# A spectral filter gated with a token MLP: reordered stages, smaller transforms, a hardware GELU

## The chip, the cores and the metric

The kernel runs on one core of a Trainium2 chip. TensorE (PE in the profile) multiplies matrices into PSUM, VectorE (DVE), ScalarE (ACT) and GpSimd (POOL) work on elements, and SyncE (SP) only issues transfers between HBM and SBUF. Each engine takes its own queue in order. The metric is the device time of one execution in microseconds: 221.72 us is the median of 4 runs of the kernel before (220.94 to 899.45).

## The reference

The input x has 2048 tokens of 512 channels. Two branches are mixed by a gate:

```
g = sigmoid(sum(x * gate_w, channels))
a = irfft2(rfft2(x) * (w_r + i w_i))                        # 2048 x 512
h = layernorm(x, channels)
b = (gelu(h^T w1 + b1) w2 + b2)^T                           # 2048 -> 1792 -> 2048, along the tokens
out = g * a + (1 - g) * b
```

`gelu` is the tanh approximation. All inputs and the output are bf16.

## The kernel before

P = 128 partitions; the tokens make NB = 16 blocks of 128, F = 1792 makes NFT = 14 column tiles.

**Branch b (dense).** Layer norm on DVE: `bn_stats` and `bn_aggr` for each block (L296, L297), one square root on ACT for all blocks (L299), a reciprocal, and a scaling for each block in place (L302). The first product (L344) makes 14 tiles `u`, each of 16 matmuls of 128 x 512 in a PSUM bank of a ring of two. GELU is done by hand: ACT adds the bias (L347), DVE forms u(u^2 + c) in two operations (L349, L350), ACT takes a sigmoid (L352), DVE multiplies (L353). The second product (L459) makes 16 tiles `yb` of 14 matmuls each, and ACT scales and biases them by 1 - g into `tbv` (L461).

**Branch a (spectral).** The two-dimensional transform is cut into stages:
- f1 (L313, L315): the real transform over the 512 channels as a product with a table `tf1`, real and imaginary part in two banks, 4 matmuls each per block. A column 256 of the table carries `gate_w`, so the gate's sums come out of the same matmuls (L319).
- a DFT of 16 over the token blocks on DVE (`fft16`): two rounds of radix-4 butterflies of one group at a time (L67 to L84), with twiddles between them (L91 to L99).
- f3 (L377 to L380): a DFT of 128 within the blocks, 4 matmuls of 256 columns for each of the 16 e, with `tce`.
- the filter (L392 to L395), four DVE operations for each e, and a small correction for the packed column (channel frequency 0 and 256 share one), which needs a permutation on TensorE (L418, L420).
- i1 (L437 to L440): the inverse DFT of 128, 8 matmuls of 128 columns for each e, with `tice`; then the inverse `fft16`; then ya (L489): the inverse over the channels, 4 matmuls of 512 columns for each block; DVE mixes it with `tbv` (L495) and the block is stored (L497).

**Tables.** `tf1`, `tce`, `tice` and `tg` are made on the chip: POOL writes index ramps, DVE multiplies them and masks the product to the period (L222), ACT takes the sine (L43).

**Order.** All transfers are issued on one SyncE queue. A planner that runs when the kernel is built orders each engine's instructions, the first in the program having priority, with later work filling gaps that it expects; on the chip the orders are fixed. A tile asks a pool for a buffer: seven "planes" of 16 KB per partition hold the large tensors in turn, PSUM has rings of two banks called pA, pB and acc. A tile that takes a buffer over waits until the last reader of the tile before it is done.

Of the kernel before, what the change touches and what calls it, by code (L numbers as in the profile page):

```python
# [9 lines left out]
Alu = mybir.AluOpType  # L10
BF16 = mybir.dt.bfloat16
F32 = mybir.dt.float32

P = 128
# [5 lines left out]
NDT = 4  # L20
F = 1792
NFT = 14
PI_BIAS = -3.1415925

GELU_C3 = 2.0 * np.sqrt(2.0 / np.pi) * 0.044715
GELU_C22 = 1.0 / 0.044715


class KernelBuilder:
    def __init__(self, ctx, tc, dbg=None):  # L30
        self.ctx = ctx
        self.tc = tc
        self.nc = tc.nc
        self.dbg = dbg or {}
        self.c_pibias = None

    def dbg_out(self, key, src_ap):
        if key in self.dbg:
            self.nc.sync.dma_start(out=self.dbg[key], in_=src_ap)

    def sin_table(self, out_ap, arg_ap, n_period):
        np_ = arg_ap.shape[0]
        self.nc.scalar.activation(  # L43
            out_ap, arg_ap, ActF.Sin, bias=self.c_pibias[0:np_], scale=2.0 * np.pi / n_period
        )


def fft16(nc, pool, in_acc, a_acc, t_acc, out_acc, inverse, tmp_shape_full, tmp_shape_half,
          eng_add=None, eng_mul=None):
    add_eng = eng_add or (lambda i: nc.vector)  # L50
    mul_eng = eng_mul or (lambda i: nc.vector)
    cnt = [0]

    def nxt():
        cnt[0] += 1
        return cnt[0]

    def bfly(us, ys):
        p = pool.tile(tmp_shape_full, BF16, tag="ffp", name="fft_p")
        q = pool.tile(tmp_shape_full, BF16, tag="ffq", name="fft_q")  # L60
        r = pool.tile(tmp_shape_full, BF16, tag="ffr", name="fft_r")
        s = pool.tile(tmp_shape_full, BF16, tag="ffs", name="fft_s")

        def half(t, comp):
            return t[:, comp] if len(tmp_shape_full) == 3 else t[:, :, comp]

        add_eng(nxt()).tensor_add(p[:], us[0][0], us[2][0])  # L67
        add_eng(nxt()).tensor_add(q[:], us[1][0], us[3][0])
        add_eng(nxt()).tensor_sub(r[:], us[0][0], us[2][0])
        add_eng(nxt()).tensor_sub(s[:], us[1][0], us[3][0])  # L70
        add_eng(nxt()).tensor_add(ys[0][0], p[:], q[:])
        add_eng(nxt()).tensor_sub(ys[2][0], p[:], q[:])
        r_re, r_im = half(r, 0), half(r, 1)
        s_re, s_im = half(s, 0), half(s, 1)
        if not inverse:
            add_eng(nxt()).tensor_add(ys[1][1], r_re, s_im)
            add_eng(nxt()).tensor_sub(ys[1][2], r_im, s_re)
            add_eng(nxt()).tensor_sub(ys[3][1], r_re, s_im)
            add_eng(nxt()).tensor_add(ys[3][2], r_im, s_re)
        else:  # L80
            add_eng(nxt()).tensor_sub(ys[1][1], r_re, s_im)
            add_eng(nxt()).tensor_add(ys[1][2], r_im, s_re)
            add_eng(nxt()).tensor_add(ys[3][1], r_re, s_im)
            add_eng(nxt()).tensor_sub(ys[3][2], r_im, s_re)  # L84

    def twiddle(src, dst, m):
        theta = 2.0 * np.pi * m / 16.0
        c = float(np.cos(theta))
        s = float(-np.sin(theta)) if not inverse else float(np.sin(theta))
        if m % 16 == 4:  # L90
            mul_eng(nxt()).tensor_scalar_mul(dst[1], src[2], -s)  # L91
            mul_eng(nxt()).tensor_scalar_mul(dst[2], src[1], s)
            return
        t1 = pool.tile(tmp_shape_half, BF16, tag="tw1", name="tw_t1")
        t2 = pool.tile(tmp_shape_half, BF16, tag="tw2", name="tw_t2")
        mul_eng(nxt()).tensor_scalar_mul(t1[:], src[2], s)
        add_eng(nxt()).scalar_tensor_tensor(dst[1], src[1], c, t1[:], op0=Alu.mult, op1=Alu.subtract)
        mul_eng(nxt()).tensor_scalar_mul(t2[:], src[2], c)
        add_eng(nxt()).scalar_tensor_tensor(dst[2], src[1], s, t2[:], op0=Alu.mult, op1=Alu.add)  # L99

    for r in range(4):
        us = [in_acc(4 * m + r) for m in range(4)]
        ys = [a_acc(4 * r + k1) for k1 in range(4)]
        bfly(us, ys)
    for r in range(1, 4):
        for k1 in range(1, 4):
            twiddle(a_acc(4 * r + k1), t_acc(3 * (r - 1) + (k1 - 1)), r * k1)
    for k1 in range(4):
        us = []
        for r in range(4):  # L110
            if r == 0 or k1 == 0:
                us.append(a_acc(4 * r + k1))
            else:
                us.append(t_acc(3 * (r - 1) + (k1 - 1)))
        ys = [out_acc(k1 + 4 * k2) for k2 in range(4)]
        bfly(us, ys)
# [3 lines left out]
def kernel(  # L120
# [12 lines left out]
    dbg=None,  # L133
    stop_after=None,
):
    kb = KernelBuilder(ctx, tc, dbg)
# [4 lines left out]
    planes = ctx.enter_context(tc.tile_pool(name="planes", bufs=7))  # L141
    tbl = ctx.enter_context(tc.tile_pool(name="tbl", bufs=1))
    small = ctx.enter_context(tc.tile_pool(name="small", bufs=1))
    psum = ctx.enter_context(tc.tile_pool(name="psum", bufs=2, space=bass.MemoryType.PSUM))

    def plane_tile(shape, name):
        return planes.tile(shape, BF16, tag="plane", name=name)

    consts = small.tile([P, 8], F32, name="consts")
    nc.vector.memset(consts[:, 0:1], PI_BIAS)  # L150
    nc.vector.memset(consts[:, 1:2], 1e-5)
    kb.c_pibias = consts[:, 0:1]
    c_eps = consts[:, 1:2]

    xn = plane_tile([P, NB, D], "xn")
    nc.sync.dma_start(out=xn[:], in_=x2.rearrange("(b a) d -> a b d", a=P))
    xt = plane_tile([P, NDT, S], "xt")
    xr = x2.rearrange("s (dt p) -> s dt p", p=P)
    for dt in range(NDT):
        nc.sync.dma_start(out=xt[:, dt], in_=xr[:, dt], transpose=True)  # L160
    wrp = planes.tile([P, NE, 258], BF16, tag="plane", name="wrp")
    wip = planes.tile([P, NE, 258], BF16, tag="plane", name="wip")
    nc.sync.dma_start(out=wrp[:, :, 0:257], in_=A_w_r.rearrange("(c e) l -> c e l", e=NE))
    nc.sync.dma_start(out=wip[:, :, 0:257], in_=A_w_i.rearrange("(c e) l -> c e l", e=NE))
    b1b = small.tile([P, NFT], BF16, name="b1b")
    nc.sync.dma_start(out=b1b[:], in_=B_b1.rearrange("(ft f) -> f ft", f=P))
    b1f = small.tile([P, NFT], F32, name="b1f")
    nc.vector.tensor_copy(b1f[:], b1b[:])
    b2b = small.tile([P, NB], BF16, name="b2b")
    nc.sync.dma_start(out=b2b[:], in_=B_b2.rearrange("(b a) -> a b", a=P))  # L170
    b2f = small.tile([P, NB], F32, name="b2f")
    nc.vector.tensor_copy(b2f[:], b2b[:])

    tf1 = tbl.tile([P, NDT, 2, 257], BF16, name="tf1")
    tce = tbl.tile([P, 3, NE, P], BF16, name="tce")
    tice = tbl.tile([P, 3, NE, P], BF16, name="tice")
    tg = tbl.tile([P, 2, 2, D], BF16, name="tg")
    pmA = tbl.tile([P, P], F32, name="pmA")
    pmB = tbl.tile([P, P], F32, name="pmB")
    nc.vector.memset(tf1[:, :, 1, 256], 0.0)  # L180
    nc.sync.dma_start(out=tf1[:, :, 0, 256], in_=gate_w.rearrange("(dt p) -> p dt", p=P))
    with tc.tile_pool(name="tgen", bufs=1) as tgp:
        I32 = mybir.dt.int32
        lam_row = tgp.tile([P, L], F32, name="lam_row")
        nc.gpsimd.iota(lam_row[:], pattern=[[1, L]], base=0, channel_multiplier=0,
                       allow_small_or_imprecise_dtypes=True)
        a_row = tgp.tile([P, P], F32, name="a_row")
        nc.gpsimd.iota(a_row[:], pattern=[[1, P]], base=0, channel_multiplier=0,
                       allow_small_or_imprecise_dtypes=True)
        d_row = tgp.tile([P, D], F32, name="d_row")  # L190
        nc.gpsimd.iota(d_row[:], pattern=[[1, D]], base=0, channel_multiplier=0,
                       allow_small_or_imprecise_dtypes=True)
        d_col4 = tgp.tile([P, NDT], F32, name="d_col4")
        nc.gpsimd.iota(d_col4[:], pattern=[[P, NDT]], base=0, channel_multiplier=1,
                       allow_small_or_imprecise_dtypes=True)
        lam_col2 = tgp.tile([P, 2], F32, name="lam_col2")
        nc.gpsimd.iota(lam_col2[:], pattern=[[P, 2]], base=0, channel_multiplier=1,
                       allow_small_or_imprecise_dtypes=True)
        ce16 = tgp.tile([P, NE], F32, name="ce16")
        nc.gpsimd.iota(ce16[:], pattern=[[1, NE]], base=0, channel_multiplier=16,  # L200
                       allow_small_or_imprecise_dtypes=True)
        pcol = tgp.tile([P, 1], F32, name="pcol")
        nc.gpsimd.iota(pcol[:], pattern=[[0, 1]], base=0, channel_multiplier=1,
# [17 lines left out]
        def and_sin(dst_bf16, arg_i32, n_period):  # L221
            nc.vector.tensor_single_scalar(arg_i32, arg_i32, n_period - 1, op=Alu.bitwise_and)  # L222
            kb.sin_table(dst_bf16, arg_i32, n_period)
# [306 lines left out]
```

## Time and profile before

The profiled execution took 899.45 us, the other three 220.94 to 222.04. Both a matmul's length and TensorE's share are those of the 899.45 us execution.

| | value |
|---|---|
| time, median of 4 | 221.72 us |
| span of the profiled execution | 897.4 us |
| TensorE busy, matmuls | 837.6 us, 826 recorded |
| DVE busy, instructions | 161.1 us, 515 |
| ACT busy, instructions | 78.3 us, 124 |
| moved by DMA | 23.23 MB |
| first steady matmuls | 56 us after the start |

A group line reads: line, engine, operation, output<-input, shape, count, then busy time and mean ns of one, then the idle time of the engine just before and what ended it. A timeline line has start, length, engine, line, operation, and what it waited for in brackets. Busy lengths of neighbours on DVE overlap a little, so the cost of one in a dense stretch is the distance of two starts.

### The profile page before, as it was taken

What the parts mean: (1) busy time and instruction counts of PE and PEld (TensorE: products, weight loads), DVE (VectorE), ACT (ScalarE), POOL (GpSimd) and SP (SyncE); (2) the same over time, 40 slices, a digit from 0 to 9 for tenths busy, and PEclk for the clock granted to TensorE, in tenths of its full rate; (3) what the DMA queues carried; (4) which work ended last, traced back from release to release, by engine and by line L of the source; (5) the groups of instructions that cost most, each with busy time, mean ns of one, the idle gap of its engine ahead of it and who ended that gap; (6) DMA issues with size and microseconds to landing.
All of it is one profiled execution on the core that took longest, in us unless ns stands there. A gap on an engine that the chain in (4) does not pass through costs nothing.

```text
span 897.4 us, 2500 instructions
## 1 busy us (share of the span) xinstructions
PE 837.6 (93%) x826; PEld 268.1 (30%) x840; DVE 161.1 (18%) x515; ACT 78.3 (9%) x124; POOL 3.8 (0%) x13
## 2 busy tenths in 40 slices
PE   0289999999999999999999999999999999999998
PEld 0044442222222222222443556522222222222221
DVE  7641111111111111110332000570000000001111
ACT  1330010000000000000111112100000000000000
POOL 1000000000000000000000000000000000000000
DMA  9630000101010101000000100011010110000000
GB/s 230 134 93 0 1 0 0 47 0 47 0 47 0 47 0 47 0 1 0 0 0 0 42 0 0 1 41 34 7 41 0 41 42 0 0 0 18 23 29 23
DMA packets 50139, 23.23 MB, mean 26 GB/s; under 512 B 13264, under 2 KB 50128, under 8 KB 50128
## 3 DMA queue, kind: packets, MB, share of 16 engines
q1 hardware_dynamic: 50128, 23.09, 10.1%
q8 instruction: 6, 0.10, 0.0%
q14 instruction: 5, 0.04, 0.0%
HBM read 18.89 MB, written 2.10 MB: 23 GB/s over the span
## 4 chain that ended last, share of the span: by engine, by line
PE 93%; SPq 3%; DVE 1%; issue 1%; ACT 1%; DMA 0%; DVEq 0%
PE u L344 32%; PE yb L459 32%; PE ya L489 9%; PE f1im L315 5%; PE f1re L313 4%; SPq L160 2%; PE i1bank L437 1%; PE i1bank L438 1%; PE f3bank L377 1%; PE i1bank L440 1%; PE f3bank L380 1%; PE f3bank L379 1%; PE i1bank L439 1%; PE f3bank L378 1%; DMA tf<-in_gate_w_dram 0%
## 5 line engine op out<-in xcount | busy, mean ns | idle before, releaser
L459 PE MATMUL yb<-glv,w2t 128*128 128x512 bf16 x216 | 294.1, 1705 | 4.7 <-issue 4.7
L344 PE MATMUL u<-xn,w1t 128*128 128x512 bf16 x219 | 291.8, 1707 | 4.7 <-issue 4.7
L344 PEld LDWEIGHTS <-w1t 128*128 128x128 bf16 x224 | 72.6, 324 | 221.6 <-issue 221.6
L459 PEld LDWEIGHTS <-w2t 128*128 128x128 bf16 x224 | 73.0, 326 | 198.6 <-issue 198.1
L313 PE MATMUL f1re<-tf,xt 128*128 128x257 bf16 x64 | 60.9, 1037 | 42.5 <-DMA tf<-in_gate_w_dram 31.0
L489 PE MATMUL ya<-tg,zt 128*128 128x512 bf16 x63 | 84.1, 1707 | 0.9 <-issue 0.9
L495 DVE SCALAR_TENSOR_TENSOR ot<-ya,g,tbv 128x512 bf16<-128x512 f32 x16 | 12.0, 751 | 282.1 <-PE ya L489 282.1
L315 PE MATMUL f1im<-tf,xt 128*128 128x256 bf16 x64 | 61.3, 1041 | 0.0
L349 DVE TENSOR_TENSOR p<-ubt 128x512 bf16<-128x512 bf16 x14 | 6.0, 426 | 246.5 <-ACT ubt L347 246.5
L489 PEld LDWEIGHTS <-zt 128*128 128x128 bf16 x64 | 20.5, 320 | 64.0 <-issue 64.0
L313 PEld LDWEIGHTS <-xt 128*128 128x128 bf16 x64 | 19.5, 307 | 64.0 <-DMA tf<-in_gate_w_dram 31.0
L347 ACT ACTIVATE ubt<-u,b1f 128x512 bf16<-128x512 f32 x14 | 9.6, 688 | 258.0 <-PE u L344 258.0
L461 ACT ACTIVATE tbv<-yb,ombb,omg 128x512 bf16<-128x512 f32 x16 | 12.4, 778 | 221.4 <-PE yb L459 221.4
L315 PEld LDWEIGHTS <-xt 128*128 128x128 bf16 x64 | 20.3, 318 | 22.1 <-issue 21.6
L437 PE MATMUL i1bank<-tice,y 128*128 128x128 bf16 x32 | 22.2, 694 | 2.3 <-ACT vp L442 1.9
L440 PE MATMUL i1bank<-tice,y 128*128 128x128 bf16 x32 | 23.0, 720 | 0.0
L439 PE MATMUL i1bank<-tice,y 128*128 128x128 bf16 x32 | 22.9, 714 | 0.0
L438 PE MATMUL i1bank<-tice,y 128*128 128x128 bf16 x32 | 22.7, 709 | 0.0
L442 ACT ACTIVATE vp<-i1bank,wlam 128x256 bf16<-128x256 f32 x32 | 13.4, 471 | 80.5 <-PE i1bank L440 80.5
L318 DVE CAST xdt<-f1im 128x256 bf16<-128x256 f32 x16 | 6.8, 424 | 62.4 <-PE f1im L315 62.4
L377 PE MATMUL f3bank<-fu,tce 128*128 128x256 bf16 x16 | 16.8, 1047 | 0.9 <-ACT xs L381 0.9
L378 PE MATMUL f3bank<-fu,tce 128*128 128x256 bf16 x16 | 16.8, 1047 | 0.0
(170 smaller groups left out, 324.2 us busy)
## 6 DMA issues: line engine op xcount, KB each, us to landing
w2t<-in_B_w_dram SPq DMA_DIRECT2D x8, 896.0 KB, 5.2
w1t<-in_B_w_dram SPq DMA_DIRECT2D x7, 1024.0 KB, 6.0
xn<-in_A_x_dram SPq DMA_DIRECT2D x1, 2048.0 KB, 8.4
out_dram<-ot SPq DMA_DIRECT2D x16, 128.0 KB, 1.7
wrp<-in_A_w_r_dram SPq DMA_DIRECT2D x1, 1028.0 KB, 6.7
wip<-in_A_w_i_dram SPq DMA_DIRECT2D x1, 1028.0 KB, 9.9
xt<-in_A_x_dram SPq DMA_TRANSPOSE x4, 6.0
b1b<-in_B_b_dram SPq DMA_DIRECT2D x1, 3.5 KB, 9.3
```

The costliest lines, as they stand in the source:

```text
L160: nc.sync.dma_start(out=xt[:, dt], in_=xr[:, dt], transpose=True)
L313: nc.tensor.matmul(pre[:, 0:257], lhsT=lhsT, rhs=tf1[:, dt, 0, :], start=(dt == 0), stop=(dt == NDT - 1))
L315: nc.tensor.matmul(pim[:, 0:L], lhsT=lhsT, rhs=tf1[:, dt, 1, 0:L], start=(dt == 0), stop=(dt == NDT - 1))
L344: nc.tensor.matmul(u[:], lhsT=w1t[:, b, q * P:(q + 1) * P], rhs=xn[:, b, :], start=(b == 0), stop=(b == NB - 1))
L377: nc.tensor.matmul(bank[:, 0:L], lhsT=tce[:, 0, e, :], rhs=ure, start=True, stop=False)
L378: nc.tensor.matmul(bank[:, 0:L], lhsT=tce[:, 1, e, :], rhs=uim, start=False, stop=True)
L437: nc.tensor.matmul(bank[:, c0:c0 + P], lhsT=blk_re, rhs=tice[:, 0, e, :], start=True, stop=False)
L438: nc.tensor.matmul(bank[:, c0:c0 + P], lhsT=blk_im, rhs=tice[:, 2, e, :], start=False, stop=True)
L439: nc.tensor.matmul(bank[:, c0 + P:c0 + 2 * P], lhsT=blk_re, rhs=tice[:, 1, e, :], start=True, stop=False)
L440: nc.tensor.matmul(bank[:, c0 + P:c0 + 2 * P], lhsT=blk_im, rhs=tice[:, 0, e, :], start=False, stop=True)
L459: nc.tensor.matmul(yb[:], lhsT=w2t[:, ft, q2 * P:(q2 + 1) * P], rhs=glv[:, ft, :], start=(ft == 0), stop=(ft == NFT - 1))
L489: nc.tensor.matmul(ya[:], lhsT=zt[:, lt, b, comp, :], rhs=tg[:, lt, comp, :], start=(i == 0), stop=(i == 3))
```

## The change

The kernel is rewritten along the same stages; the purpose is less work on TensorE and DVE, and an earlier start. What it does:

- **Head.** x is loaded in four pieces, and the first six column tiles of w1 right after the first piece. Layer norm goes block by block, with a square root for each block, and the six tiles accumulate in six banks at once, block by block as they are normed. The transposed x for f1 comes after these loads.
- **f1** uses the symmetry of the transform: sums and differences of the two channel halves (`xf`) give even and odd frequencies, so that a block needs 4 matmuls of 256 columns. Evictions alternate between ACT and DVE. ya uses the same symmetry: even and odd parts in the two halves of a bank, ACT scales them by the gate, DVE adds and subtracts.
- **The gate** has its own sums: DVE multiplies x with a broadcast `gate_w`, ACT adds up along the channels; the sigmoid is taken as a tanh.
- **GELU** is one ACT activation per tile.
- **fft16** works on four groups at a time, with whole-tile operations of 2048 elements, and folds some twiddles into the butterflies. The filter works on four e at a time.
- **f3** and **i1** use wider matmuls: one of 512 and two of 256 columns for an e, and 4 of 256 for an e in i1.
- **Tables**: the products of ramps for `tce` and `tice` are made on POOL in quarters. The masks stay on DVE, the sines on ACT.
- **Buffers**: each large tensor has a fixed plane; `vp` takes the plane of `hn`, `wri` that of the table ramp `rec`. The dense product has six banks, everything else shares two. Weights of both products share four buffers.

The core of the diff:

```diff
-    psum = ctx.enter_context(tc.tile_pool(name="psum", bufs=2, space=bass.MemoryType.PSUM))
+    psum = ctx.enter_context(tc.tile_pool(name="psum", bufs=6, space=bass.MemoryType.PSUM))
+    home = {"x": 0, "fa": 0, "xs": 0, "ia": 0, "hn": 1, "vp": 1, "zt": 1, "xt": 2, "xdt": 2, "fu": 2, "ap": 2,
+            "marg": 3, "xf": 3, "y": 3, "rec": 4, "wri": 4, "marg3": 5, "gl": 5, "prod": 6, "tbv": 6}
...
+    for b0, b1 in ((0, 2), (2, 6), (6, 11), (11, 16)):
+        nc.sync.dma_start(out=x[:, b0:b1], in_=xv[:, b0:b1])
+        if b0 == 0:
+            load_w1a(0)
+    for g in range(1, 4):
+        load_w1a(g)
...
+    u1 = [mm_bank(f"u1_{ft}") for ft in range(FT1)]
+    for b in range(NB):
+        nc.vector.bn_stats(out=stats[:, b, :], in_=x[:, b, :])
+        nc.vector.bn_aggr(out=mv[:, b, :], in_=stats[:, b, :])
+        sq = nc.scalar.activation(rstd[:, b:b + 1], mv[:, b, 1:2], ActF.Sqrt, bias=consts[:, 1:2], scale=1.0)
+        nc.vector.reciprocal(rstd[:, b:b + 1], rstd[:, b:b + 1])
+        nc.vector.tensor_scalar(hn[:, b, :], x[:, b, :], mv[:, b, 0:1], rstd[:, b:b + 1],
+                                op0=Alu.subtract, op1=Alu.mult)
+        for ft in range(FT1):
+            nc.tensor.matmul(u1[ft][:], lhsT=w1a[b // 4][:, b % 4, ft * P:(ft + 1) * P], rhs=hn[:, b, :],
+                             start=(b == 0), stop=(b == NB - 1))
+    with tc.issue_after(sq.ins):
+        nsin(tf[:, :, :, 0, :], m1c.rearrange("p k (t i) -> p k t i", t=2), 512)
...
+        nc.gpsimd.tensor_scalar(m2[:, es], rec[:, es], dcol[:, 0:1], 0.0, op0=Alu.mult, op1=Alu.add)
+        nc.gpsimd.tensor_scalar(m2c[:, es], rec[:, es], dcol[:, 0:1], 1536.0, op0=Alu.mult, op1=Alu.add)
...
+        nc.vector.tensor_add(xf[:, 0, :, hs], xt[:, 0:2, hs], xt[:, 2:4, hs])
+        nc.vector.tensor_sub(xf[:, 1, :, hs], xt[:, 0:2, hs], xt[:, 2:4, hs])
...
-            ubt = gwork.tile([P, D], BF16, tag="ub", name="ubt")
-            nc.scalar.activation(ubt[:], u[:], ActF.Identity, bias=b1f[:, ft:ft + 1], scale=1.0)
-            p2 = gwork.tile([P, D], BF16, tag="p2", name="p2")
-            nc.vector.tensor_mul(p2[:], ubt[:], ubt[:])
-            nc.vector.scalar_tensor_tensor(p2[:], p2[:], GELU_C22, ubt[:], op0=Alu.add, op1=Alu.mult)
-            sg = gwork.tile([P, D], BF16, tag="sg", name="sg")
-            nc.scalar.activation(sg[:], p2[:], ActF.Sigmoid, scale=GELU_C3)
-            nc.vector.tensor_mul(glv[:, ft, :], ubt[:], sg[:])
+            nc.scalar.activation(gl[:, ft, :], u[:], ActF.Gelu_apprx_tanh, bias=b1f[:, ft:ft + 1], scale=1.0)
...
-    for r in range(4):
-        us = [in_acc(4 * m + r) for m in range(4)]
-        ys = [a_acc(4 * r + k1) for k1 in range(4)]
-        bfly(us, ys)
+    stage([x[:, 4 * m:4 * m + 4] for m in range(4)], "a", emit_a)
...
+        nc.tensor.matmul(bank[:], lhsT=tce[:, 0, e, :], rhs=fu[:, e].rearrange("p c l -> p (c l)"),
+                         start=True, stop=False)
+        nc.tensor.matmul(bank[:, 0:L], lhsT=tce[:, 1, e, :], rhs=fu[:, e, 1], start=False, stop=False)
+        nc.tensor.matmul(bank[:, L:2 * L], lhsT=tce[:, 2, e, :], rhs=fu[:, e, 0], start=False, stop=True)
...
+                nc.tensor.matmul(o, lhsT=y[:, e, 0, par:L:2], rhs=tice[:, e, 1:3].rearrange("p t a -> p (t a)"),
+                                 start=True, stop=False)
+                nc.tensor.matmul(o, lhsT=y[:, e, 1, par:L:2], rhs=tice[:, e, 0:2].rearrange("p t a -> p (t a)"),
+                                 start=False, stop=True)
...
-        nc.vector.scalar_tensor_tensor(ot[:], ya[:], g[:, b:b + 1], tbv[:, b, :],
-                                       op0=Alu.mult, op1=Alu.add)
+        nc.vector.tensor_add(ot[:], tbv[:, b], ap_[:, b].rearrange("p t d -> p (t d)"))
```

## The prediction

> **What bounds the kernel now.** I read the totals, the chain that ended last, the waits, the head of the timeline, and then dense stretches for the price of one operation.
>
> ```profile
> PE 837.6 (93%) x826; PEld 268.1 (30%) x840; DVE 161.1 (18%) x515; ACT 78.3 (9%) x124; POOL 3.8 (0%) x13
> ```
>
> ```profile
> 31.03 5.31 PE f1re L313 x8
> ...
> 56.23 5.27 PE f1im L315 x8
> ...
> 132.72 65.11 PE u L344 x49
> ```
>
> The chain's columns are start, length, work. 49 matmuls of 512 columns in 65.11 us are 1.33 us each; 448 of them would be 595 us, which doesn't fit into the timed 221.72 us. This execution ran TensorE several times slower than the timed ones, so its TensorE times can't be used, nor its shares. Durations of DVE, ACT and DMA can, and so can everything up to 56 us, where TensorE hardly works:
>
> ```profile
> PE f1re L313 <- DMA tf<-in_gate_w_dram: 31.0, 1, 31.0
> PE f1re L313 <- DVE glog L319: 11.5, 1, 11.5
> ```
>
> ```profile
> 0.74 0.46 SPq L156 DMA_DIRECT2D xn<-in_A_x_dram  x1
> 1.26 15.85 SPq L160 DMA_TRANSPOSE xt<-in_A_x_dram  x4
> 17.15 0.66 SPq L163 DMA_DIRECT2D wrp<-in_A_w_r_dram  x1
> ```
>
> TensorE starts at 31 us, when a 1 KB load lands that stands in the one queue behind x, its transposes and the filter, stops again behind DVE's tables and layer norm, and runs steadily only from 56. So the head costs 56 us. The price of DVE work is the distance of starts in a dense stretch:
>
> ```profile
> 590.73 0.41 DVE L71 TENSOR_TENSOR zt<-fft_p,fft_q 128x512 bf16<-128x512 bf16 x1
> 591.06 0.41 DVE L72 TENSOR_TENSOR zt<-fft_p,fft_q 128x512 bf16<-128x512 bf16 x1
> 591.40 0.28 DVE L81 TENSOR_TENSOR zt<-fft_r,fft_s 128x256 bf16<-128x256 bf16 x1
> 591.60 0.28 DVE L82 TENSOR_TENSOR zt<-fft_r,fft_s 128x256 bf16<-128x256 bf16 x1
> ```
>
> 512 elements take 0.336, 256 take 0.201: 0.066 fixed plus 0.527 ns an element. Hence 1024 cost 0.61 and 2048 cost 1.15 us. From the groups I take ACT's prices:
>
> ```profile
> L347 ACT ACTIVATE ubt<-u,b1f 128x512 bf16<-128x512 f32 x14 | 9.6, 688 | 258.0 <-PE u L344 258.0
> L461 ACT ACTIVATE tbv<-yb,ombb,omg 128x512 bf16<-128x512 f32 x16 | 12.4, 778 | 221.4 <-PE yb L459 221.4
> L381 ACT CAST xs<-f3bank 128x512 bf16<-128x512 f32 x16 | 9.4, 586 | 45.4 <-PE f3bank L380 45.4
> ```
>
> And the early rate of the transfers (0 to 9 us the plain x, 9 to 17 us the transposes; last column GB/s):
>
> ```profile
> 0.00:9.00 9.00, 0.00 (x0) 0.00 (x0) 6.73 (x23) 2.43 (x2) 3.76 (x13) 1.00 0.83 250
> 9.00:17.00 8.00, 0.00 (x0) 0.00 (x0) 7.87 (x18) 2.00 (x1) 0.00 (x0) 1.00 1.07 192
> ```
>
> **What the skill says.** The Trainium skill, "TensorE: Matmul & The Clock Gate", Part 1, gives N/2.4 GHz plus 2.5 ns for a warm matmul (216 ns at 512 columns) and half that clock for the first 3.4 us of activity. This trace disagrees (1.33 us), but the timed 221.72 us needs something near it: from 56 us on 166 us are left for some 324,000 columns, at most 0.51 ns a column. So a 512-column matmul costs 216 to 262 ns in timed runs; I take 216. "VectorE: DVE Perf Modes", the perf-mode tier table, has 1224 ns for a bf16 tensor_tensor of 2048; my slope gives 1.15 between starts, which agrees. "ScalarE: Activation LUTs", What ACT_TABLE_LOAD costs, has 1283 ns; the trace shows 1283.
>
> **Check on the old kernel.** It streams 448 x 512 (the two dense products) + 32,832 (f1) + 16,384 (f3) + 16,384 (i1) + 32,768 (ya) = 327,744 columns in 832 matmuls: 136.6 + 2.1 = 138.7 us. Head 56.2, TensorE afterwards 136.9 (16 matmuls fall before), last eviction and store 3.3 (894.09 to 897.4), 2.0 outside the span (899.45 against 897.4): 198.4. Measured 221.7, so 23 us of holes. About 10 I can place: the 16 weight groups keep DVE for 17.3 us beside 15 us of queued TensorE work, with a 2 us permutation behind them; the 32 evictions L442 of 0.47 us pace i1; f1 waits on two buffers. Some 13 us, 9% of the TensorE work, stay unexplained; the new kernel gets the same surcharge.
>
> **The change part by part.**
> TensorE: the dense products stay at 229,376 columns; f1, f3, i1 and ya are 64, 48, 64 and 64 matmuls of 16,384 columns per stage. Sum 294,912 columns in 688 matmuls, 124.6 us: 14.1 less.
>
> Head: x (2.1 MB) and the first six columns of W1 (3.1 MB) go first. The first window moved 250 GB/s including some 2 us before anything landed, so about 326 GB/s after that: 16 + 2 = 18 us. Then 2.1 MB of transposes at 192 GB/s: 11 us, 29, landed about 30. Meanwhile layer norm runs per block on DVE: bn_stats 0.62 + aggregate 0.08 + reciprocal about 0.1 + scaling 0.34 = 1.15, x16 = 18.4, with 4 us of table arguments: done at about 26. The 96 early matmuls (20.7 us, 1.7 more while the clock is low) follow block by block and end at about 27. This moves 20.7 us of TensorE work into time that was idle. The first xf pair (2 x 1.15) after the transposes lets f1 start at 32, where the old one got going at 56.
>
> f1: 6.9 us of TensorE, but only two banks. A bank's round is 0.43 matmul + 0.65 eviction (ACT 0.59, DVE about 0.69) + about 0.3 of signals, so 0.7 per block: 11 us, f1 ends at 43. The second part of W1 can hardly fill this: its six banks hold the early sums until their GELUs run, and those stand on ACT behind the sines (from 26: table load 1.28, four of about 0.7, four of 2.0: 38 us, then another table load).
>
> GELU: 14 x (0.34 + 0.60 + 0.34) = 18 us leave DVE, and 14 sigmoids leave ACT; one 0.69 us activation per tile remains. Beside the u tiles DVE had 18 + 30 us against 48 of TensorE, so this is slack won rather than time.
>
> DFT of 16: before, four stage groups of 2.82, twiddles 7.8 and again 11.3: 30.4 us. Now stage a: five of 2048 (5.75), one of 1024, one of 512, two of 256 (1.35), four of 1024 (2.4): 9.5. Stage b: 6 x 1.15 + 2.4 = 9.3. Twiddles: about 5.1 by the same slope. 23.9 us, twice: 13 us less DVE work. Weights: 16 x 1.08 = 17.3 become 4 x 3.5 = 14. Output: 16 x 0.68 become 16 x 0.34, after 16 x 0.40 of sum and difference.
>
> New DVE and ACT work with an answer at once: four gate products (4.6) and the masks lie in f1's and the layer norm's gaps; 16 accumulating copies on ACT (0.6 each) lie beside the DFT. Table arguments on Pool: the trace before shows only iotas there (2048 elements 1.91 us, so 0.56 for 512). "GPSIMD Engine Reference", Performance versus the Vector engine, has 4.5 us for a two-input operation on 2048: an estimate of 1.1 for 512. Twenty such: 11 to 23 us; I take 20. They are needed at f3, near 63, so they cost nothing.
>
> New waits: vp takes over the buffer of hn, so i1's evictions wait until every matmul of the second W1 part is done. 128 matmuls, 27.6 us from about 43: 73 with stray stalls. The forward DFT ends at 43 + 24 = 67, weight group 0 needs 3.5 more: i1 would start at 71. Near zero. The W1 remainder needs buffers that the early matmuls free from 13 us on and queues behind the transposes: 4 MB at about 290 GB/s, first piece at 34. Hidden.
>
> The spectral chain alone: 43 + DFT 24 = 67; weights 14 + packed column 4 = 85; last half of i1, 8 x 0.75 = 91; inverse DFT 24 = 115; last ya blocks 8 x 0.75 = 121. TensorE alone from 32: 124.6 - 20.7 = 104, and 1.7 for the clock: 138. TensorE ends later, by 17 us, because the second product (48.4 us) fills the chain's waits. Tail: 0.78 + 0.34 + about 2.0 for the store = 3.1, outside 2.0. Sum 143. Holes at 9% of 104 us, as in the old kernel: 9, of which f1's two banks are 4. Together 152.
>
> **Rivals.**
> 1. The order on TensorE is fixed ahead, so it may stand behind waits of the spectral chain instead of filling them. If nothing of the second product fills, 121 + 48.4 + 5 = 174; half, 163. For it: the trace shows matmuls of yb put between those of f3 in an order that only fits one set of speeds. Against: six banks for the dense product, and 17 us slack.
> 2. The head stays: Pool, or a sine behind a wait, holds f1 until 56 as now. 56 + 104 + 5 = 165. For it: DVE takes turns, and a mask waiting for Pool would hold the layer norm behind it. Against: 20 us of Pool work.
> 3. Slower than before: f1 would have to start at 221.7 - 109 = 113 us, or Pool's tables reach f3 at 160 (f3 to the end is about 61). That is 8 us per Pool operation of 512: 224 us. Only the absence of such a row before speaks for it.
>
> **How the numbers follow.** Forecast (140 to 160, TensorE filled) 0.60; rival 1 (160 to 176) 0.23; rival 2 0.11; rival 3 0.03; under 139 or between 176 and 221, 0.03. Predicted 152. Low 139 is first matmul at 7 + 124.6 + 5, rounded up, no holes. High 172 holds most of rivals 1 and 2, and is also what 262 ns a matmul would give: 152 + 0.21 x 104 = 174. Faster 0.96, same 0.01, slower 0.03.
>
> **What would show it.** First matmul near 7 us; f1 at about 32; 688 bf16 matmuls plus four small f32 groups; DVE busy near 125 us with no GELU work; the chain ending in yb, tbv, the last add and store. If TensorE idles in front of f3, i1 or ya with yb still left, rival 1 holds; if f1 starts after 45, rival 2. Wrong altogether if Pool or a buffer wait appears in the chain.

## The result, and the profile after

The changed kernel takes 161.68 us (median of 11 runs, 160.66 to 162.63) against 221.66 us: a ratio of 0.7295, 95% interval [0.7272, 0.7318]. The forecast was 152.0, in a range of 139 to 172. The first profile of the kernel before is of an execution of 899.45 us; where the old kernel's TensorE is read below, its second profile is used, that of the first experiment.

The totals, and the slices of the span (3.98 us each) for TensorE, DVE and the granted clock, of the kernel after:

```profile
PE 135.9 (86%) x683; PEld 68.9 (43%) x696; DVE 123.3 (78%) x286; ACT 83.9 (53%) x146; POOL 22.4 (14%) x32
...
PE   0091999996499999998999999999997999999980
...
DVE  1659999999977999999999990499999989612111
...
PEclk9998579999879999999999999999999999999999
```

Nearly everything the forecast said of the body holds: TensorE is full from the twelfth slice on (but for the one before ya, near 122 us), DVE is at 123 us (forecast: near 125), Pool at 22 (20). The chain that ended last closes as foreseen, in the second dense product; the columns are start, length and work:

```profile
122.85 1.05 PE ya L443 x8
...
140.81 10.96 PE yb L470 x50
151.82 2.77 PE yb L470 x12
154.61 0.79 ACT tbv L472
```

50 matmuls of 512 columns in 10.96 us are 0.2192 each. What differs is the head. TensorE's timeline:

```profile
8.20 4.37 PE L229 MATMUL u<-hn,w1a 128*128 128x512 bf16 x12 [8.20 <-DMA w1a<-in_B_w_dram]
16.11 21.04 PE L229 MATMUL u<-hn,w1a 128*128 128x512 bf16 x83 [3.54 <-DVE hn L226]
37.95 0.61 PE L291 MATMUL f<-tf,xf 128*128 128x256 bf16 x4 [0.80 <-DVE xf L284]
39.09 0.61 PE L291 MATMUL f<-tf,xf 128*128 128x256 bf16 x4 [0.52 <-DVE xf L285]
41.73 1.02 PE L457 MATMUL u<-hn,w1b 128*128 128x512 bf16 x2 [2.03 <-ACT gl L304]
```

After the first two blocks TensorE stops until 16.1; f1 starts at 38.0 (forecast 32) and waits for `xf`; the rest of the first product waits for the first GELU and starts at 41.7. DVE's timeline shows why. It has no gap between 10 and 42 us:

```profile
9.59 1.28 DVE L222 BATCH_NORM_STATS2 stats<-x 128x6 f32<-128x512 bf16 x2 [2.91 <-DMA x<-in_A_x_dram]
...
11.51 0.35 DVE L211 TENSOR_SCALAR m1t<-lrow,dcol 128x256 int32<-128x256 f32 x1
11.77 1.13 DVE L212 TENSOR_SCALAR m1t<-lrow,dcol 128x256 int32<-128x256 f32 x1
...
15.37 0.69 DVE L226 TENSOR_SCALAR hn<-x,mv,rstd 128x512 bf16<-128x512 bf16 x1
...
31.27 3.48 DVE L195 TENSOR_SCALAR marg<-marg 128x2048 int32<-128x2048 int32 x3
...
36.69 1.21 DVE L284 TENSOR_TENSOR xf<-xt 128x2048 bf16<-128x2048 bf16 x1
```

x's second piece lands only at 9.6, behind the first weights in the queue. Then the arguments of tf's sines stand ahead of the third block, at up to three times their first length, and delay its scaling to 15.4; and four masks (29.5 to 34.7), a negation and a gate product stand ahead of `xf`. On ACT the sines end at 39.7, a table load follows, and the first GELU runs at 41.0. The waits that matter, with total us, times, longest:

```profile
PE u L229 <- DVE hn L226: 3.5, 1, 3.5
...
DVE pa L38 <- ACT vp L431: 4.4, 1, 4.4
...
PE u L457 <- ACT gl L304: 2.0, 1, 2.0
...
ACT vp L431 <- PE u L457: 1.8, 1, 1.8
```

### The profile page after: what moved, and what is told of

It reads as the page before. It is cut to its first block, busy times and chain, and to the rows that moved or that the text cites. A ratio compares the mean times of both kernels' runs of the same rounds, so it can differ in the third digit from the quotient of the medians.

```text
span 159.0 us, 2001 instructions
## 1 busy us (share of the span) xinstructions
PE 135.9 (86%) x683; PEld 68.9 (43%) x696; DVE 123.3 (78%) x286; ACT 83.9 (53%) x146; POOL 22.4 (14%) x32
## 4 chain that ended last, share of the span: by engine, by line
DVE 50%; PE 35%; ACT 5%; DMA 5%; issue 1%; SPq 1%; DVEq 0%; ACTq 0%
PE yb L470 16%; PE ya L443 5%; DVE stats L222 5%; DMA x<-in_A_x_dram 5%; PE u L457 4%; PE f L291 3%; DVE hn L226 3%; PE f L379 3%; DVE marg L195 2%; ACT junk L317 2%; DVE pa L38 2%; DVE pb L38 2%; DVE qa L40 1%; DVE xf L285 1%; DVE xf L284 1%; DVE sb L41 1%
## 5 line engine op out<-in xcount | busy, mean ns | idle before, releaser
L470 PE MATMUL yb<-gl,w2t 128*128 128x512 bf16 x217 | 50.3, 379 | 0.3
L229 PE MATMUL u<-hn,w1a 128*128 128x512 bf16 x95 | 25.4, 434 | 11.8 <-DMA w1a<-in_B_w_dram 8.2
L457 PE MATMUL u<-hn,w1b 128*128 128x512 bf16 x123 | 31.3, 387 | 2.2 <-ACT gl L304 2.0
L470 PEld LDWEIGHTS <-w2t 128*128 128x128 bf16 x224 | 21.9, 98 | 23.1
L472 ACT ACTIVATE tbv<-yb,ombb,omg 128x512 bf16<-128x512 f32 x16 | 12.5, 778 | 27.6 <-PE yb L470 27.6
L229 PEld LDWEIGHTS <-w1a 128*128 128x128 bf16 x96 | 10.3, 109 | 26.3 <-issue 9.6
L457 PEld LDWEIGHTS <-w1b 128*128 128x128 bf16 x128 | 12.7, 100 | 14.0 <-issue 2.5
L222 DVE BATCH_NORM_STATS2 stats<-x 128x6 f32<-128x512 bf16 x16 | 10.5, 664 | 5.6 <-DMA x<-in_A_x_dram 5.6
L446 ACT ACTIVATE eo<-ya,gs 128x512 bf16<-128x512 f32 x16 | 10.3, 688 | 4.5 <-PE ya L443 2.2
L443 PEld LDWEIGHTS <-zt 128*128 128x128 bf16 x64 | 6.1, 97 | 5.3 <-DVE zt L97 1.7
L427 PE MATMUL i<-tice,y 128*128 128x256 bf16 x32 | 7.7, 271 | 0.4 <-ACT vp L431 0.2
L429 PE MATMUL i<-tice,y 128*128 128x256 bf16 x32 | 7.7, 272 | 0.0
```

Source lines behind the costliest of these rows:

```text
L222: nc.vector.bn_stats(out=stats[:, b, :], in_=x[:, b, :])
L229: nc.tensor.matmul(u1[ft][:], lhsT=w1a[b // 4][:, b % 4, ft * P:(ft + 1) * P], rhs=hn[:, b, :], start=(b == 0), stop=(b == NB - 1))
L443: nc.tensor.matmul(bank[:, par * L:(par + 1) * L], lhsT=zt[:, b, comp, par, :], rhs=tg[:, par, comp, :], start=(comp == 0), stop=(comp == 1))
L446: nc.scalar.activation(eo[:], bank[:].rearrange("p (t d) -> p t d", t=2), ActF.Copy, scale=gs[:, b:b + 1])
L457: nc.tensor.matmul(u[:], lhsT=w[:, b, k * P:(k + 1) * P], rhs=hn[:, b, :], start=(b == 0), stop=(b == NB - 1))
L470: nc.tensor.matmul(yb[:], lhsT=w[:, ft, k * P:(k + 1) * P], rhs=gl[:, ft, :], start=(ft == 0), stop=(ft == NFT - 1))
```

## Experiments

**1. The kernel before again**, unchanged.

> The kernel before, unchanged, for a profile in which a matmul of 512 columns takes its 0.22 us. Theory (the prediction's reconstruction): steady matmuls from 56 us, f1 done at about 71, the tiles u until about 122, the filter and i1 until about 161, inverse DFT to about 190, ya until about 210, with TensorE idle for some 23 us between 56 us and the end. Rival (TensorE is not the bound after 56 us but DVE is): DVE busy over 95% from 71 to 190 us, and TensorE idle for 40 us or more of it.

222.07 us, ratio 1.0018 [0.9992, 1.0045]. Its windows give start:end and length, then busy time of PE, PEld, DVE, ACT and POOL, clock, DMA share, GB/s:

```profile
71.00:122.00 51.00, 50.66 (x241) 23.87 (x245) 46.63 (x154) 17.90 (x30) 0.00 (x0) 1.00 0.39 104
122.00:145.00 23.00, 14.35 (x90) 9.28 (x92) 20.66 (x83) 9.92 (x19) 0.00 (x0) 0.93 0.14 40
```

The hand GELU lies in the first window, where TensorE is full: DVE has slack there, 46.6 of 51. The old kernel's holes are in the second, around f3 and the filter (8.65 us without TensorE), and in its last 20 us, where pairs of blocks leave every 2.6 us because two output buffers go round:

```profile
197.54 3.76 PE L489 MATMUL ya<-tg,zt 128*128 128x512 bf16 x16
```

```profile
201.22 1.61 DVE L495 SCALAR_TENSOR_TENSOR ot<-ya,g,tbv 128x512 bf16<-128x512 f32 x2 [1.01 <-DMA out_dram<-ot]
203.85 1.59 DVE L495 SCALAR_TENSOR_TENSOR ot<-ya,g,tbv 128x512 bf16<-128x512 f32 x2 [1.02 <-DMA out_dram<-ot]
```

ya's last matmul ends at 217.0, 19.4 us after the first began, for 14.0 us of work (64 of 0.2192). So of the 23 us of holes that the forecast counted in the old kernel, 8.7 are around f3 and the filter and 5.4 in the output ring. About 2 more are no holes: a 512-column matmul costs 0.2192 us and not 0.216. Some 7 us are not placed. The rival, DVE as the bound, is refuted: from 71 to 190 us DVE is busy for 98 of 119 us, and TensorE idle for only 9.5.

**2. Hardware GELU in the kernel before.**

```diff
-            ubt = gwork.tile([P, D], BF16, tag="ub", name="ubt")
...
-            nc.vector.tensor_mul(glv[:, ft, :], ubt[:], sg[:])
+            nc.scalar.activation(glv[:, ft, :], u[:], ActF.Gelu_apprx_tanh, bias=b1f[:, ft:ft + 1], scale=1.0)
```

> One part alone: the kernel before with GELU as one activation per tile; 42 DVE operations (18 us) and 14 activations fewer. Theory (slack rather than time, since TensorE's 48 us of tiles u cover DVE's work beside them): 216 to 221 us. Rival (DVE shares the bound beside the tiles u): the forward DFT ends 15 us earlier and the time falls to 203 to 210.

220.16 us, ratio 0.9943 [0.9917, 0.9969]: 18 us of DVE work gone, about 1.3 us gained. In the old kernel it is slack, as the forecast said.

**3. The hand GELU in the kernel after.** The five instructions of the old kernel replace the activation in both places; the sigmoid is written over p2, and the output has two buffers instead of three, for space.

> One part undone: the changed kernel with GELU by hand again (the bias, three DVE operations and a sigmoid per tile; the output ring has two buffers in place of three to make room). DVE gets 18 us more, 11 of them beside the forward DFT. Theory (after 42 us TensorE is the bound, and 18 us of the second product are left when ya ends): at most 3 us more, 162 to 165. Rival (the spectral chain on DVE sets the end): 10 to 18 us more, 172 to 180.

189.25 us, ratio 0.8525 [0.8471, 0.8579]: 27.6 us slower than the kernel after, more than both theories. Waits, then ACT's timeline:

```profile
ACT ubt L308 <- DVE gl L313: 9.4, 3, 8.2
...
PE yb L482 <- DVE gl L313: 5.8, 1, 5.8
```

```profile
118.01 0.67 ACT L312 ACTIVATE p<-p 128x512 bf16<-128x512 bf16 x1
126.92 0.69 ACT L308 ACTIVATE ubt<-u,b1f 128x512 bf16<-128x512 f32 x1 [8.24 <-DVE gl L313]
```

The sigmoid is done at 118.7, but its product `gl` stands in DVE's queue behind the inverse DFT's first operations and runs at 126.5; only then has the next tile a buffer. Each tile of the second product sums over all 14 `gl`, so none can finish before the last, at 146.7 instead of 89.6 in the kernel after. From 120 to 140 TensorE works 11.9 us of 20. The loss has two parts. The chain itself is held by the work that DVE has got back: f3 begins at 82.1 instead of 75.8, the inverse DFT at 116.6 instead of 101.6, and what is left of the second product after ya starts at 155.8 instead of 136.3, 19.5 us later. And more is left: 127 matmuls against 82. The 45 more are 9.9 us, work that should have filled the chain's waits. The two add up to the 29.2 us between the two profiled executions. So GELU off DVE isn't slack in the new kernel: it shortens the chain, and it takes an operand of what fills TensorE off the chain's queue. The output's two buffers are not the cause: the last 127 matmuls run at 0.222 us each.

**4. One fourteenth of the second product.** Each `yb` has 1 matmul instead of 14: 13 of 14 terms of the second dense product are left out, 45 us of TensorE.

```diff
-            for ft in range(NFT):
+            for ft in range(13, NFT):
```

> The changed kernel with only the last of 14 matmuls in each of the 16 tiles yb: 208 matmuls of 512 columns, 45 us of TensorE, are left out, so the dense branch's output is partial. What remains is the spectral chain with the first product beside it. Theory (the second product fills the chain's waits and its end sticks out): the chain is unchanged, ya ends near 134 and the time is 135 to 142, so 45 us of removed work save only 20 to 27. Rival (TensorE is the bound throughout and the chain has much slack): 117 to 125.

149.84 us, ratio 0.6741 [0.6688, 0.6793]: some 12 us less, where the forecast had 135 to 142 us and the rival still less. Windows, and TensorE's timeline:

```profile
110.00:122.00 12.00, 0.00 (x0) 0.00 (x0) 11.76 (x31) 0.93 (x2) 0.00 (x0) 0.58 0.00 0
122.00:130.00 8.00, 3.49 (x16) 2.28 (x17) 8.00 (x10) 1.37 (x2) 0.00 (x0) 0.50 0.00 0
```

```profile
126.51 3.68 PE L443 MATMUL ya<-tg,zt 128*128 128x256 bf16 x16 [19.96 <-DVE zt L97]
```

TensorE idles 20 us under the inverse DFT. So the kernel without this filling takes about 12 us less, and the forecast had 17 between the chain and the end of TensorE. The chain is not quite undisturbed here. ya ends at 140.8, against 136.4 in the kernel after and 134 expected. The inverse DFT begins 3.7 us later (105.3 against 101.6), as activations for `tbv` now stand among i1's evictions on ACT. And the granted clock is 0.50 in ya's first 3.7 us; in the kernel after, where TensorE is busy up to ya, it is 1.00 there.

**5. Early dense matmuls behind f1 in the program.**

```diff
-        for ft in range(FT1):
-            nc.tensor.matmul(u1[ft][:], lhsT=w1a[b // 4][:, b % 4, ft * P:(ft + 1) * P], rhs=hn[:, b, :],
-                             start=(b == 0), stop=(b == NB - 1))
...
+    for b in range(NB):
+        for ft in range(FT1):
+            nc.tensor.matmul(u1[ft][:], lhsT=w1a[b // 4][:, b % 4, ft * P:(ft + 1) * P], rhs=hn[:, b, :],
+                             start=(b == 0), stop=(b == NB - 1))
```

> The kernel after with the 96 early matmuls of the dense product put behind f1 in the program instead of behind each layer norm block. Theory (TensorE is the bound from 38 us on, and the early start moved 20.7 us of its work into time that was idle): 176 to 183 us against 161.7. A smaller loss is possible where the moved matmuls fill f1's eviction pauses. Rival (the chain of the spectral branch on DVE sets the end, since that kernel without its second product still took 149.8): at most 168 us.

161.21 us, ratio 0.7288 [0.7252, 0.7325]. It decides nothing: the planner put the matmuls back into the idle time of the head (83 of them from 15.9 us on). What a program's order says and what the queue holds are two things. Experiment 9 forces the order.

**6. xf first.** `marg` goes to plane 6, and the block that forms `xf` ahead of the masks.

```diff
-            "marg": 3, "xf": 3, "y": 3, "rec": 4, "wri": 4, "marg3": 5, "gl": 5, "prod": 6, "tbv": 6}
+            "marg": 6, "xf": 3, "y": 3, "rec": 4, "wri": 4, "marg3": 5, "gl": 5, "prod": 6, "tbv": 6}
```

> The kernel after with the table argument marg in plane 6 instead of the plane that xf takes over, and xf ahead of the masks of tce and tice. Theory (f1 started at 38 instead of 32 us because the masks and the buffer that waits for tce's sines stood in front of xf): f1 starts at 32 to 34, and the time falls by 3 to 5 us, to 157 to 159 us. Rival (the sines now come later and hold the first GELUs on ACT, and with them the banks for the rest of the dense product): 160.5 to 164 us with f1 at 34 all the same.

162.19 us, ratio 0.7341 [0.7297, 0.7386]. TensorE:

```profile
16.81 21.03 PE L229 MATMUL u<-hn,w1a 128*128 128x512 bf16 x83 [3.81 <-DVE hn L226]
37.68 1.04 PE L291 MATMUL f<-tf,xf 128*128 128x256 bf16 x8
...
48.00 0.63 PE L457 MATMUL u<-hn,w1b 128*128 128x512 bf16 x1
```

f1 starts no earlier. `xf` is begun at 32.3 instead of 36.7, but now f1 waits for TensorE itself, which is with the early matmuls until 37.8. And the rival is right on ACT: the sines come 5 us later, the first GELU at 47.2, the rest of the first product at 48.0 instead of 41.7.

**7. Layer norm first.** The arguments of tf's sines go behind the layer norm.

```diff
-    m1t = tmp.tile([P, 2, 2, 2 * P], I32, tag="ffp", name="m1t")
...
     with tc.issue_after(sq.ins):
```

> The kernel after with the arguments of tf's sines (eight DVE instructions) behind the layer norm instead of in front of it. Theory (they ran at a third of their speed while Pool worked, and held the layer norm behind them): layer norm ends 2 to 3 us earlier, at 25 to 26.5, the early matmuls end near 34, and the time falls by 1.5 to 3 us, to 158.7 to 160.2. Rival (DVE has the same work in front of xf in either order, so f1 starts where it did): 161 to 162.5 us.

162.37 us, ratio 0.7320 [0.7272, 0.7367]. The early matmuls run without the stop and end at 32.0, but f1 starts at 39.2, since the same DVE work stands ahead of `xf`. Layer norm ends at 28.5, not at the 25 to 26.5 expected. Nor is the contention gone. The groups of the kernel after, and then of this one:

```profile
L226 DVE TENSOR_SCALAR hn<-x,mv,rstd 128x512 bf16<-128x512 bf16 x16 | 6.9, 428 | 0.1
...
L211 DVE TENSOR_SCALAR m1t<-lrow,dcol 128x256 int32<-128x256 f32 x2 | 1.5, 736 | 0.0
```

```profile
L215 DVE TENSOR_SCALAR hn<-x,mv,rstd 128x512 bf16<-128x512 bf16 x16 | 9.8, 630 | 0.1
...
L227 DVE TENSOR_SCALAR m1t<-lrow,dcol 128x256 int32<-128x256 f32 x2 | 0.7, 348 | 0.0
```

The arguments are back at 348 ns; now the scalings beside Pool have become slow.

**8. Copies instead of the DFTs of 16**: the transform's arithmetic is left out, eight copies stand for it, twice.

```diff
-    fft16(nc, tmp, xdt[:], fa[:], fu[:], inverse=False)
+    for r in range(4):
+        nc.vector.tensor_copy(fa[:, r], xdt[:, 4 * r:4 * r + 4])
+    for r in range(4):
+        nc.vector.tensor_copy(fu[:, 4 * r:4 * r + 4], fa[:, r])
```

> The kernel after with each DFT of 16 replaced by eight copies of 2048 elements per partition: the transform's arithmetic is left out, the output is not the reference's. Some 30 us of DVE work leave the chain. Theory (TensorE is the bound; 103 us of columns stand between 41.7 and the end, and some 10 us of holes that the chain leaves): 151 to 157 us. Rival 1 (the chain is as long as TensorE's work): below 148 us. Rival 2 (the holes come from the clock and from banks, not from the chain): 159 to 162.5 us.

158.76 us, ratio 0.7180 [0.7138, 0.7221]. DVE falls from 123.3 to 86.5 us, the time by 2.9. From 60 us on TensorE works over 97% of every 10 us up to 150. So it sets the end, and the chain's pauses are worth about 3 us. 158.76 lies above the forecast's 151 to 157, just below the rival that puts the holes down to the clock and the banks. The clock has its part in the head: from 40 to 50 us TensorE works 7.78 of 10 us, with a granted clock of 0.67.

**9. Early dense matmuls forced behind f1.**

```diff
+    with tc.issue_after(mm.ins):
+        for b in range(NB):
+            for ft in range(FT1):
+                nc.tensor.matmul(u1[ft][:], lhsT=w1a[b // 4][:, b % 4, ft * P:(ft + 1) * P], rhs=hn[:, b, :],
+                                 start=(b == 0), stop=(b == NB - 1))
```

> The kernel after with the 96 early matmuls of the dense product ordered behind the last matmul of f1 on TensorE's queue, so that they can't be filled in earlier. Theory (TensorE's work from f1 on sets the end, and the early start moved 20.7 us of it into time that was idle): f1's 6.9 us of matmuls stand alone for some 11 us, then 117 us of columns follow with 6 to 10 us of holes, so 174 to 182 us. Rival (the spectral chain sets the end): at most 168 us.

191.84 us, ratio 0.8660 [0.8609, 0.8711]: 30.2 us lost for 20.7 us of matmuls that moved. TensorE, and its wait in f1:

```profile
37.98 2.17 PE L287 MATMUL f<-tf,xf 128*128 128x256 bf16 x8 [37.98 <-DVE xf L280]
42.19 2.84 PE L287 MATMUL f<-tf,xf 128*128 128x256 bf16 x12 [2.03 <-ACT xdt L290]
...
51.21 5.54 PE L287 MATMUL f<-tf,xf 128*128 128x256 bf16 x24 [0.81 <-ACT xdt L290]
...
57.99 20.88 PE L300 MATMUL u<-hn,w1a 128*128 128x512 bf16 x96
...
96.47 22.61 PE L459 MATMUL u<-hn,w1b 128*128 128x512 bf16 x104
```

```profile
PE f L287 <- ACT xdt L290: 5.3, 5, 2.0
```

f1 alone takes from 38.0 to 58.2, where 11 us were expected; the difference is most of what the forecast of 174 to 182 us lacks. Its 64 matmuls are busy for 14.9 us, 0.23 each, against 0.11 from start to start in the kernel after, and 5.3 us go on waits for ACT's evictions. That is the rate of a halved clock: in experiment 7, f1's first eight matmuls, after 7.3 us without one, also take 2.17 us, with a granted clock of 0.50, against 1.04 in experiment 6, where f1 follows without a pause. But the clock on record for this execution is 1.00 throughout, so the cause stays open. After f1, TensorE is busy for 122.3 of 127 us.

The order costs something else, which does not show in the time. `vp` takes the buffer of `hn`, so i1's evictions can't begin before the first product has read `hn` for the last time. TensorE's queue has 104 of those matmuls in one piece, with i1 and the packed column's product behind them, so DVE waits for 21.0 us. TensorE works through all of this wait (22.00 of 22 us from 97 to 119), so it loses nothing there. That the planner put them in one piece because of this buffer is argued, not shown. Altogether the early start is worth 30 us against this order: 20.7 are the work itself. That most of the rest comes from other matmuls ahead of f1's and between them, which this order doesn't have, is argued.

**10. Tables after f1.** Experiment 7's edit, the tables with their masks and sines behind f1 and the first GELUs in the program, and buffers that don't hold up `xf` (`marg` in plane 6, `marg3` in 4). Nothing is left out. On the chip two of tce's masks are still ahead of `xf`, at 27.5 and 29.2, as the planner put them back.

```diff
-    mask(m2, 2048)
-    nsin(tce[:, 2], m2, 2048)
...
+    mask(m3c, 2048)
+    nsin(tice[:, :, 1, :], m3c, 2048)
     nc.vector.tensor_scalar_mul(tce[:, 1], tce[:, 2], -1.0)
```

> The kernel after with the table work moved in time and nothing left out: tf's arguments behind the layer norm, the tables tg and tice (DVE arguments, masks, ACT sines) behind f1 and the first GELUs in the program, and the table arguments in buffers that xf doesn't take over. Theory (DVE's queue, full from 10 to 42 us, sets f1's start, and the sines on ACT set the first GELU): f1 starts at 33 to 35 and the first of the rest of the dense product at 36 to 38, and the time falls by 4 to 7 us, to 155 to 158 us. Rival (the moved work comes back as evictions of f1 that wait on DVE and ACT; f1 ends near 55 as before): 160 to 163 us.

158.88 us, ratio 0.7162 [0.7119, 0.7205]: 2.8 us less than the kernel after, just above the forecast of 155 to 158.

```profile
32.00 0.38 PE L272 MATMUL f<-tf,xf 128*128 128x256 bf16 x2 [1.16 <-ACT tf L198]
32.75 0.83 PE L272 MATMUL f<-tf,xf 128*128 128x256 bf16 x6 [0.37 <-DVE xf L266]
36.87 1.01 PE L272 MATMUL f<-tf,xf 128*128 128x256 bf16 x4 [3.29 <-DVE xdt L278]
```

f1 starts at the forecast's 32.0; 3.3 us are lost again, because the second bank's eviction stands on DVE behind all of `xf` and a mask.

**11. Pool later.** As experiment 10, with Pool's eight operations for tice behind a one-column copy of the last layer norm result.

```diff
+    gate = nc.gpsimd.tensor_copy(late[:], rstd[:, NB - 1:NB])
+    with tc.issue_after(gate.ins):
```

> The kernel of the run before it (tables after f1) with Pool's eight operations for tice ordered behind the last square root of the layer norm, so that Pool is idle while layer norm runs. Theory (DVE instructions of the faster kind run at half speed or less beside Pool's arithmetic): the scaling of a block takes 0.40 us from the third block on instead of 0.4 to 1.0, layer norm ends 2 to 3 us earlier than in that run, and the time falls by a further 1 to 3 us. Rival (no contention: the scaling is as slow without Pool, or the gain is lost since tice's masks now wait for Pool in DVE's queue with f1's evictions behind them): the same time within 1 us, or slower.

162.80 us, ratio 0.7345 [0.7313, 0.7376]: 3.9 us slower than experiment 10. The groups of experiment 10, then of this one:

```profile
L215 DVE TENSOR_SCALAR hn<-x,mv,rstd 128x512 bf16<-128x512 bf16 x16 | 8.3, 536 | 0.1
L266 DVE TENSOR_TENSOR xf<-xt 128x2048 bf16<-128x2048 bf16 x2 | 2.4, 1222 | 0.0
```

```profile
L215 DVE TENSOR_SCALAR hn<-x,mv,rstd 128x512 bf16<-128x512 bf16 x16 | 6.3, 407 | 0.1
L269 DVE TENSOR_TENSOR xf<-xt 128x2048 bf16<-128x2048 bf16 x2 | 3.7, 1840 | 0.0
```

Both are right in part: layer norm ends 2.1 us earlier without Pool (24.8 against 26.9), and Pool then slows `xf`, one operation of it to 2.06 us. The contention isn't removed by moving Pool's work but put on whatever DVE does meanwhile, and DVE waits 2.0 us more for tice's products. Which instructions it hits isn't settled: in the kernel after most scalings ran at 0.39 beside the same Pool instructions.

**12. The first evictions.** Experiment 10, with the bias cast between the two halves of `xf`, and the second f1 bank evicted by ACT.

```diff
-        if b % 2 == 0:
+        if b % 2 == 0 or b == 1:
```

> The kernel with the tables after f1 (158.9 us), and two more edits: the cast of the first product's bias goes between the two halves of xf instead of behind them, so that ACT's table load and first GELU needn't wait for it, and ACT takes the second f1 bank as well as the first, so that no eviction stands behind xf and a mask on DVE. Theory (TensorE waits 3.3 us for that eviction and starts the rest of the dense product 1.3 us late): the first matmul of the rest comes near 36 us instead of 37.7, and the time falls by 1 to 2 us, to 157 to 158 us. Rival (the start no longer counts, since TensorE's later pauses take up whatever is won): 158.4 to 159.4 us.

155.50 us, ratio 0.7004 [0.6970, 0.7038], the best version: the kernel after has 0.7295 [0.7272, 0.7318], so this is 4.0% faster.

```profile
31.90 0.38 PE L275 MATMUL f<-tf,xf 128*128 128x256 bf16 x2 [1.16 <-ACT tf L198]
...
35.80 1.46 PE L458 MATMUL u<-hn,w1b 128*128 128x512 bf16 x3 [2.32 <-DMA w1b<-in_B_w_dram]
```

The rest of the first product starts at 35.8, 5.9 us earlier than in the kernel after, and the time falls by 6.2. Against experiment 10 it is 3.4 us, more than the 1 to 2 that were expected; which of the two edits brings how much isn't separated. The next wait is for w1b's load, 2.3 us, which the forecast called hidden.

## Why the prediction was right, and where it missed

The forecast's case held: TensorE sets the end, and the second product fills the chain's waits. Its sum was 32 + 104 + 1.7 + 9 + 5.1 = 151.8; the profiled execution took 160.8, 0.9 less than the median. Term by term:

- **f1 was to start at 32: it started at 38.0, so 6.0 us too early.** This is the step that failed, in three places. (a) The gate products and masks were to "lie in f1's and the layer norm's gaps": DVE has no gap from 10 to 42 us, so every mask is an addition. A row of 1.14 us (2048 integers) times four is most of the 6 us. (b) f1 needed TensorE as well as `xf`. The early matmuls were to end at 27; they ended at 37.1, because TensorE stopped at 12.6 until the third block came at 16.1 behind the sine arguments, and the 84 that were left are 18.4 us by themselves, at a granted clock of 0.74 from 10 to 20 us and 0.91 from 20 to 30. (c) The forecast names no buffer wait ahead of `xf`, but `xf` takes over the plane of `marg` and so waits for tce's sines, which end at 35.9. Experiment 6 removes three of the four masks in (a), and (c); experiment 7 removes the stop in (b); neither gains anything. Experiment 10 removes the stop, the buffer wait and two of the four masks, and f1 starts at 32.0.
- **TensorE from f1 on, 114.7: 116.6 measured** (38.0 to 154.6), 1.9 more. The surcharge of 9 us for holes held in size but not for its reason. At 0.2192 us for 512 columns, the work from f1 on is 105.2 us, so 11.4 are holes and slow matmuls, against 10.7 in the forecast. Those of the old kernel that it came from lie in good part around f3 and in the output ring (experiment 1). Those of the new one lie before 60 us by about half: TensorE is idle for 2.8 us from 38 to 60 and works at a clock of 0.92; from 60 to 154 it is idle for 3.2. And with next to no DFT arithmetic on DVE only 2.9 us went (experiment 8). That a surcharge taken from other causes had the right size is luck.
- **Tail, 5.1: 6.2 measured** (154.6 to the end of the span at 159.0, and 1.8 outside), 1.1 more.

6.0 + 1.9 + 1.1 = 9.0, which with 151.8 is all of the 160.8.

Right: 294,912 columns at 216 ns for 512 (0.2192 measured); DVE at 1.15 us for 2048 elements (1.14); layer norm 1.15 a block (1.04 where undisturbed); Pool's 20 us (22.4), with a two-input product of 512 at 1.06 to 1.13 (the estimate was 1.1). The `vp` wait, "near zero", is 1.8 us in the kernel after; without the early start of the first product, i1's first banks were full at 96.5 and the first eviction ran at 119.1 (experiment 9).

**f1 was to end at 43: its last bank was read at 56.1.** It cost little, since matmuls of the first product stood between f1's. But the chain began its DFT that much later, and ended ya at 136.4 instead of 121, so the estimate of the chain was some 15 us short. That this didn't reach the sum is in part luck: the 17 us by which TensorE was to end later took it up. TensorE did end 18.2 us after ya, though with the second product taken out only some 12 us went (experiment 4).

**"Slack won rather than time", for GELU**, was right for the kernel before (1.3 us) and wrong for the kernel after (27.6), where it lengthened the chain by 19.5 us and left 9.9 us of the filling for the end (experiment 3). It was judged in the profile of before, where GELU stands beside TensorE work that doesn't need it. In the new order, its result is what the filling work waits for.

**Pool "cost nothing"** needed more than that it ends in time. The Trainium skill, "SBUF — State Buffer", section Who interferes with whom, says that VectorE and GpSimd share a port pair as an exclusive lock. The trace agrees in kind: 0.35 us became 1.13 beside Pool (kernel after); a scaling of layer norm takes 0.41 on average without Pool and 0.54 with it (experiments 11 and 10), an addition or subtraction for `xf` 1.22 without and 1.84 with it (10 and 11). The forecast looked up what a Pool operation costs, and not whom it holds up.

Rival 1 is refuted in the kernel after: from 60 us on, TensorE's longest wait for the chain is the 1.2 us for `zt` ahead of ya. It describes experiment 3 well. Rival 2 went the right way: the head held f1, until 38 instead of 56.

## What to carry to other kernels

Before writing that work lies in an engine's gaps, add up that engine's queue over the stretch in question: a start time is the sum of all that stands ahead of it, on every engine and buffer that it needs, and removing one of three equal holders gains nothing. Take the work that fills another engine's waits off the queue that makes those waits. And when an engine is called idle enough to take over work, ask which ports it shares with the one that is full.

## What the runs showed that was not expected

- Pool's tensor_scalar on 512 elements takes 1.95 us from integers to integers and 0.69 from f32 to integers, both beside DVE's work; it was moved to Pool to relieve DVE and held DVE up there.
- Beside DVE's work Pool is slowed as well: a pair of integer products took 2.1 us beside layer norm (experiment 10) and 3.5 beside `xf` (experiment 11).
- With TensorE idle for 20 us the granted clock fell to 0.58 and to 0.50 in the next 8 us (experiment 4); in the kernel after, where the second product fills that pause, it was 1.00 at ya. So work that fills a pause can also keep the clock for what follows.
- ACT's accumulating copy is two instructions, 0.63 and 0.19 us.
